# Batches of 10, 8 and 6 units, a fifth early unit of the last stage, and another way to fetch the fallback's rows

## The chip, the cores and the metric

One core of one Trainium2 chip runs the whole kernel in one launch. The metric is the device time of that launch in microseconds. Engines: TensorE (PE, its weight loads PEld), VectorE (DVE), ScalarE (ACT), GpSimd (POOL) and SyncE (SP), which issues the plain transfers; the indirect ones are issued by GpSimd.

## The reference, cut to what matters

```python
# 1 attention: B, H, S, D = 4, 8, 768, 48
for t in range(S):
    state = alpha[:, :, t, :, None] * state + np.einsum('bhd,bhe->bhde', k[:, :, t], v[:, :, t])
    y[:, :, t] = np.einsum('bhd,bhde->bhe', q[:, :, t], state)
# 2 experts on x, 3072 tokens of 384; 8 experts, 1024 hidden
do_compute = x @ w_skip > 0
xc = x[do_compute]; logits = xc @ w_gate; e_idx = np.argmax(logits, axis=1)
# gate_w: the softmax probability of e_idx
y[mask] = gate_w[mask, None] * (np.maximum(xc[mask] @ w1[e], 0.0) @ w2[e])   # for each e, mask = e_idx == e
out = x.copy(); out[do_compute] = xc + y
# 3 last stage on all tokens, 2048 hidden
h = x @ w_in; g = h - np.tanh(h); return g @ w_out
```

The weights of the last stage come in 64-bit floats, all else in 32-bit floats.

## The kernel before, in words

The kernel has three stages, attention, experts and last stage, in an order that is written out by hand: each engine runs its instructions in the order in which the lines below issue them, and waits on semaphores in that order. Nothing is replanned.

**Attention** goes over 24 units of 128 tokens (6 chunks of each of 4 sequences). Step s of `astep` works on several units: loads for s + 4, VectorE's two scans for s + 2 (`scanF`, `scanG`), the score product and its mask for s (`mmA`, `mask`), the output products of s - 1 (`mmYs`, `mmYa`), and the transposition of s - 2 back to token rows with its skip and gate logits (`evx`, `mmX`, `evxa`). Whatever else is to run beside a step is listed by step, in `at` (ahead of the step) and `aft` (behind its mask).

**Routing** is done for batches of units, 11, 9 and 4. `route1` (two pieces) finds the argmax, `route2` and `evr` count tokens ahead of each token on TensorE and copy the counts out, `route1b` fills gate and id, `route3` makes the row numbers (`loc`). `scatter(u)` then writes the unit's 128 rows with an indirect transfer into `xb`: 256 rows for each expert, then the tokens that skip the experts from the front of a second area and the others from its back.

**The transition.** The first 512 skipping tokens (`rload(0)`, step 21) need no expert. For them the last stage's first NE0 = 4 of 16 hidden units are computed between attention and the experts. `split2(0, a)` transposes 128 of those rows and splits them into two parts of TensorE's rounded 32-bit format, a high (ScalarE's cast) and a low one (VectorE's difference). Each weight unit is split in the same way: `wsplit` has two pieces for an expert's unit, and for the last stage's 64-bit weights five (s0 to s3): a mask-and-shift and a merge on VectorE, two ScalarE copies with a VectorE mask between, and three VectorE passes. All 64-bit units share one buffer (`raw64`). `mm1b` is a unit's first product (9 matmuls of 512 columns) and returns the steps behind it: tanh on ScalarE, g on VectorE, g's high part on ScalarE, its low part on VectorE. `mm2b` is the second product (12 matmuls of 384 columns). Between the units the first weights of expert 0 are split (RING0 = 4 buffers, loaded through three raw buffers).

**Experts.** 8 experts of 8 units each, `mm1` and `mm2`, with later weights loaded and split three to five units ahead. The same stage splits the last stage's units 4 to 9, which stay resident. **The last stage** runs the 12 other units for block 0 and all 16 for blocks 1 to 5, 92 steps, with the last NLATE = 6 weights split in its first steps.

**The fallback**, behind the last stage, is skipped unless an expert got over 256 tokens or too few tokens skip (`bounds`, `flag`). It computes every token anew from the rows fetched by `loc`.

Lines that the steps name: L235 score product, L240 mask, L256 output product, L303 and L311/L312 rows back and out, L155 to L176 split of 64-bit weights, L141/L144 split of expert weights, L386 and L393 rank product and its copy, L424 scatter, L438 rload, L446 to L449 transposes and splits, L473 and L507 the last stage's products, L479 to L485 tanh, g, high part, low part, L521 scatter to the output, L569 an expert's first product, L934 the skipped block, L1052 the end.

Of the kernel before, what the change touches and what calls it, by code (L numbers as in the profile page):

```python
# [39 lines left out]
RING = 8  # L40
LA = RING - 3
RAWS = 5
NE0 = 4
NLATE = 6

# [5 lines left out]
TOP = NS + N - 1  # L53
NROWS = NS + N
NCL = NE + 2
BATCHES = (11, 9, 4)
NB = max(BATCHES)
XW = PD + 9

# [2 lines left out]
def tile_kernel(ctx: ExitStack, tc: tile.TileContext, att0, att, vt, wsg, wmoe, wff, out):  # L62
# [229 lines left out]
    def evx(u):  # L292
        d = U[u]
        d["xT"] = rt.tile([PR, NP, C], F32, tag="xT", name=f"xT{u}")
        (V.tensor_copy if u == NU - 1 else A.copy)(d["xT"], d["py"])

    def mmX(u):

        d = U[u]
        d["px"] = (ps["T"].tile([128, NP, 128], F32, tag="X", name=f"px{u}") if u < NU - 1 else  # L300
                   ps["T"].tile([128, 2, NP, C], F32, tag="A", name=f"px{u}")[:, 0])
        for p in range(NP):
            T.matmul(d["px"][:, p, :XW], d["xT"][:, p], selw[:, p], start=p == 0, stop=p == NP - 1)  # L303
# [118 lines left out]
    def scatter(u):  # L422
        k, i = where[u]
        s_ = nc.gpsimd.indirect_dma_start(  # L424
            xb[:, :], bass.IndirectOffsetOnAxis(loc[:, u:u + 1], 0), RT[k]["xr"][:, i, :], None,
            bounds_check=NROWS - 1, oob_is_err=False)
        if u:
            tc.declare_no_dep(s_.ins, group="route", reason="rows of their own")
        tc.add_to_no_dep_group("route", s_.ins)
# [32 lines left out]
    def mm1b(nb, f, psum=psY):  # L462

        d = X2[nb]
        wh, wl = w_t[NMU + f]
        hp = psum(f"h2_{nb}_{f}")
        todo = [(w_[:, 128 * k:128 * k + 128], x_[:, k])
                for k in range(KT) for w_, x_ in ((wh, d["h"]), (wl, d["h"]), (wh, d["l"]))]
        last = len(todo) - 1

        def issue(n=len(todo)):
            for _ in range(min(n, len(todo))):
                T.matmul(hp, *todo.pop(0), start=len(todo) == last, stop=not todo)  # L473

        def after():
            g = rings["g"].tile([128, 512], F32, tag="g", name=f"g{nb}_{f}")
            gh = rings["g"].tile([128, 512], F32R, tag="gh", name=f"gh{nb}_{f}", bufs=3)
            gl = rings["g"].tile([128, 512], F32R, tag="gl", name=f"gl{nb}_{f}", bufs=3)
            A.activation(g, hp, AF.Tanh)  # L479
            yield  # L480
            V.tensor_tensor(g, hp, g, ALU.subtract)  # L481
            yield
            A.copy(gh, g)  # L483
            yield
            V.tensor_tensor(gl, g, gh.bitcast(F32), ALU.subtract)  # L485
            d["g", f] = (gh, gl)

        return issue, after
# [206 lines left out]
        at[s].append(lambda r0=r0: nc.sync.dma_start(  # L695
            xb[r0:r0 + 512, :].rearrange("(a p) d -> p a d", a=4), zero.unsqueeze(1).to_broadcast([128, 4, RW])))

    for k, (ld, s0) in enumerate(((1, 4), (6, 8), (12, 16), (19, 0))):
        at[ld].append(lambda k=k: wload(NMU + k))
        early = wsplit(NMU + k, fine=True)  # L700
        if s0:
            for s, f_ in zip((0, 1, 1, 2, 3), early):
                aft[s0 + s].append(f_)
    route = [route1(c) for c in range(len(BATCHES))]

    def advance(c):
# [2 lines left out]
    def rank(c, psum):  # L709
        route2(c, psum)  # L710
        evr(c)

    ranks = {first[1] + 3: 0, NU - 1: 1}
    for s, c, f_ in ((first[1] + 1, 0, advance), (first[1] + 2, 0, advance), (first[1] + 3, 0, route1b),
                     (first[1] + 4, 0, route3),
                     (NU - 3, 1, advance), (NU - 2, 1, advance), (NU - 1, 1, route1b), (NU - 1, 1, route3)):
        aft[s].append(lambda c=c, f_=f_: f_(c))
    for i in range(BATCHES[0]):
        aft[15 + (i + 1) // 2].append(lambda i=i: scatter(i))
    at[21].append(lambda: rload(0))  # L720

    def astep(s):

        def ok(u):
            return 0 <= u < NU

        def pX_(name):
            return ps["T"].tile([128, 512], F32, tag="X", name=name)

        if ok(s + 4):  # L730
            aload(s + 4)
        if ok(s + 3):
            vload(s + 3)
        for f_ in at[s]:
            f_()
        mmA(s)
        if ok(s - 2):
            evx(s - 2)
        if s in ranks:
            rank(ranks[s], pX_)  # L740
        if ok(s + 2):
            scanF(s + 2)
            mkqh(s + 2)
            scanG(s + 2)
            mkkh(s + 2)
            mkpf(s + 2)
        if ok(s - 1):
            mmYs(s - 1)
        trk(s)
        if ok(s - 1):  # L750
            evst(s - 1)
        evk(s)
        if ok(s - 2):
            mmX(s - 2)
            evxa(s - 2)
        mask(s)
        if ok(s - 1):
            mmYa(s - 1)
        for f_ in aft[s]:
            f_()  # L760
        mmS(s)
# [5 lines left out]
    p0 = pool("p0", 1)  # L767
    rings["x2", 0] = p0
    last = len(BATCHES) - 1
    aft[NU - 1].append(lambda: [scatter(u) for u in range(first[1], first[last])])  # L770
    for s in (NU - 2, NU - 1):
        a = 2 * (s - NU + 2)
        aft[s].append(lambda a=a: split2(0, a))
        aft[s].append(early[s - NU + 2])
        astep(s)
        split2(0, a + 1)


    def pX(name):
# [4 lines left out]
    mmYa(NU - 1)  # L784
    evx(NU - 1)
    mmX(NU - 2)
    evxa(NU - 2)
    mmX(NU - 1)
    evxa(NU - 1)
    early[2]()  # L790
    early[3]()
    att_ctx.close()
    rings["raw"] = pool("raws", 3, route_ctx, "right")
    part = p0.tile([128, 4, DM], F32, name="part")
# [17 lines left out]
    evr(last)  # L812
    route1b(last)
    route3(last)
    early[4]()
    for u in range(first[last], NU):
        scatter(u)
    psT_ctx.close()
    ps["A"] = pool("psA", 2, ps_ctx, space=bass.MemoryType.PSUM)
    next(fill[0])  # L820
# [1 line left out]
    more(psY)  # L822
    more(psS)
    for f in range(NE0):
        if 0 < f < NE0 - 3:
            more(psS)
        next(fill[f])
        next(fill[f])
        if f + 2 < NE0:
            next(fill[f + 2])  # L830
        next(fill[f], None)
        if f == NE0 - 1:
            for f_ in wsplit(f):
                f_()
            route_ctx.close()
            rings["ring2"] = pool("ring2", RING - RING0, moe_ctx, "right")
            rings["xe"] = pool("xe", 3, moe_ctx, "right")
            rings["m2"] = pool("m2", 2, moe_ctx, "right")
            rings["raw"] = pool("raws2", RAWS, moe_ctx, "right")
            xload(0)  # L840
            xload(1)
            wload(RING0)
            for a in range(2):
                xprep(0, a)
            for f_ in wsplit(RING0):
                f_()
        mm2b(0, f)
        if f < NE0 - 1:
            for f_ in wsplit(f):
                f_()  # L850
    blk0.close()
    at, aft = collections.defaultdict(list), collections.defaultdict(list)

# [80 lines left out]
    with tc.If(past > 0):  # L934
        xd = dp.tile([NU, 128, RW], F32, name="xd")
        xa = fp.tile([128, RW], F32, name="xa")
        for u in range(NU):
            nc.gpsimd.indirect_dma_start(xa, None, xb[:, :], bass.IndirectOffsetOnAxis(loc[:, u:u + 1], 0))
            nc.sync.dma_start(xd[u], xa)
        ecur = fp.tile([128, 1], F32, name="ecur")  # L940
        acc = fp.tile([128, DM], F32, name="acc")
        xTd = fp.tile([128, KT, 128], F32, name="xTd")
# [113 lines left out]
```

## Time and profile before

| | us |
|---|---|
| median of 3 runs | 725.51 (725.43 to 726.36) |
| the profiled execution | 726.17 |
| its span, first to last instruction | 724.5 |
| TensorE busy | 681.0 (94%) |
| VectorE, ScalarE, GpSimd busy | 439.4, 301.0, 144.1 |
| mean granted TensorE clock | 0.987 |

The page also cuts the span in 40 slices. TensorE's busy tenths are given in 40 digits on the page; below nine tenths are the first slice, four between 109 and 181 us, and the last. A busy TensorE is one with matmuls in flight; the ends of matmuls are modelled, so starts are the surer times. In the timeline the bracket behind a row says how long the engine had been idle and what ended that.

### The profile page before, as it was taken

How to read it: one execution, taken by the hardware profiler on the slowest of the kernel's cores; microseconds unless marked ns; L12 is line 12 of the kernel's file. 1: busy time of each engine (PE TensorE's matmuls, PEld its weight loads, DVE VectorE, ACT ScalarE, POOL GpSimd, SP SyncE). 2: the span in 40 equal slices, each digit the busy share in tenths (PEclk: the TensorE clock that was granted, in tenths of full speed). 3: DMA queues.
4: the chain of work that ended last, by engine and by line, in shares of the span. 5: the costliest groups of instructions: out<-in, count | busy, mean ns of one | idle time of the engine just before them, and what ended most of it. 6: DMA issues, size and time to landing. Idle time of an engine off the chain costs nothing.

```text
span 724.5 us, 11897 instructions
## 1 busy us (share of the span) xinstructions
PE 681.0 (94%) x4707; PEld 627.1 (87%) x4707; DVE 439.4 (61%) x712; ACT 301.0 (42%) x587; POOL 144.1 (20%) x145
## 2 busy tenths in 40 slices
PE   4999998868999999999999999999999999999993
PEld 3899997757999999989888999999989999999892
DVE  8999999756888888859943334333333343333331
ACT  2565563325666666525532333233323332333220
POOL 6665589250011111110011002000200020001002
PEclk9999999989999999999999999999999999999997
DMA  9999876347678877512210011001100110001001
GB/s 278 199 220 292 210 187 188 129 147 263 203 261 283 266 261 261 157 61 87 88 58 32 0 31 58 0 1 45 45 0 1 46 43 1 1 1 43 1 1 47
DMA packets 30543, 81.40 MB, mean 112 GB/s; under 512 B 4405, under 2 KB 14677, under 8 KB 30480
## 3 DMA queue, kind: packets, MB, share of 16 engines
q1 hardware_dynamic: 26384, 68.64, 32.1%
q0 software_dynamic: 4096, 11.92, 4.5%
q8 instruction: 39, 0.64, 0.4%
q14 instruction: 24, 0.20, 0.1%
HBM read 65.45 MB, written 15.84 MB: 112 GB/s over the span
## 4 chain that ended last, share of the span: by engine, by line
issue 52%; PE 17%; DVE 3%; POOL 2%; DMA 1%; ACT 0%; POOLq 0%; SPq 0%; ACTq 0%
PE hp L569 8%; PE yp L587 3%; PE yp L588 3%; PE yp L589 3%; POOL out_dram L521 2%; DVE wl L144 1%; PE pe L446 1%; DMA raw<-in_wmoe_dram 0%; DVE xe L596 0%; DVE ca L156 0%; DVE hl L574 0%; DVE ca L169 0%; DVE cl L165 0%; DVE el L449 0%; DVE cs L155 0%
## 5 line engine op out<-in xcount | busy, mean ns | idle before, releaser
L481 DVE TENSOR_TENSOR g<-h,g 128x512 f32<-128x512 f32 x96 | 66.3, 691 | 158.1 <-ACT g L479 149.8
L507 PE MATMUL y<-wh,gl 128*128 128x384 f32 x384 | 130.0, 339 | 0.1
L507 PE MATMUL y<-wh,gh 128*128 128x384 f32 x384 | 129.7, 338 | 0.4 <-ACT gh L483 0.4
L507 PE MATMUL y<-wl,gh 128*128 128x384 f32 x384 | 129.7, 338 | 0.0
L479 ACT ACTIVATE g<-h 128x512 f32<-128x512 f32 x96 | 57.3, 598 | 167.9 <-PE h L473 167.9
L473 PE MATMUL h<-xh,wl 128*128 128x512 f32 x288 | 114.2, 397 | 6.8 <-DVE wl L176 6.8
L473 PE MATMUL h<-xh,wh 128*128 128x512 f32 x288 | 115.6, 401 | 1.2 <-DVE g L481 1.2
L473 PE MATMUL h<-xl,wh 128*128 128x512 f32 x288 | 114.2, 396 | 0.0
L485 DVE TENSOR_TENSOR gl<-g,gh 128x512 fp32r<-128x512 f32 x96 | 66.5, 692 | 59.5 <-ACT gh L483 40.3
L521 POOL DMA_INDIRECT out_dram<-ob,id x24 | 23.7, 986 | 370.8 <-DVE ob L520 308.1
L483 ACT CAST gh<-g 128x512 fp32r<-128x512 f32 x96 | 59.6, 621 | 89.3 <-DVE g L481 89.3
L507 PEld LDWEIGHTS y<-wh,gh 128*128 128x128 f32 x384 | 72.1, 188 | 4.6 <-ACT gh L483 0.7
L507 PEld LDWEIGHTS y<-wl,gh 128*128 128x128 f32 x384 | 72.2, 188 | 4.2
L507 PEld LDWEIGHTS y<-wh,gl 128*128 128x128 f32 x384 | 72.1, 188 | 0.9 <-DVE gl L485 0.9
L473 PEld LDWEIGHTS h<-xh,wl 128*128 128x128 f32 x288 | 54.6, 190 | 16.3 <-DVE wl L176 7.6
L473 PEld LDWEIGHTS h<-xl,wh 128*128 128x128 f32 x288 | 54.5, 189 | 12.5
L141 ACT CAST wh<-raw 128x768 fp32r<-128x768 f32 x64 | 53.4, 835 | 26.7 <-PE yp L589 23.2
L473 PEld LDWEIGHTS h<-xh,wh 128*128 128x128 f32 x288 | 54.4, 189 | 10.3 <-DVE g L481 1.6
L144 DVE TENSOR_TENSOR wl<-raw,wh 128x768 fp32r<-128x768 f32 x64 | 60.7, 949 | 3.9 <-ACT wh L141 3.8
L569 PE MATMUL hp<-eh,wh 128*128 128x256 f32 x192 | 56.2, 293 | 3.8 <-DVE hl L574 3.8
L569 PE MATMUL hp<-el,wh 128*128 128x256 f32 x192 | 54.1, 282 | 0.2 <-DVE el L449 0.2
L569 PE MATMUL hp<-eh,wl 128*128 128x256 f32 x192 | 54.1, 282 | 0.0
(141 smaller groups left out, 1144.8 us busy)
## 6 DMA issues: line engine op xcount, KB each, us to landing
raw<-in_wmoe_dram SPq DMA_DIRECT2D x64, 384.0 KB
raw<-in_wff_dram SPq DMA_DIRECT2D x16, 768.0 KB
it<-in_att_dram SPq DMA_DIRECT2D x40, 289.5 KB
rows<-xb SPq DMA_DIRECT2D x6, 776.0 KB
vt<-in_vt_dram SPq DMA_DIRECT2D x24, 192.0 KB
xb<-zero SPq DMA_DIRECT2D x4, 776.0 KB
xe<-xb SPq DMA_DIRECT2D x8, 388.0 KB
it<-in_att_dram SPq DMA_DIRECT2D x2, 772.0 KB
```

The lines of the kernel that those rows point to most:

```text
L141: A.copy(t_["h"], raw_t[i])
L144: V.tensor_tensor(t_["l"], raw_t[i], t_["h"].bitcast(F32), ALU.subtract)
L473: T.matmul(hp, *todo.pop(0), start=len(todo) == last, stop=not todo)
L479: A.activation(g, hp, AF.Tanh)
L481: V.tensor_tensor(g, hp, g, ALU.subtract)
L483: A.copy(gh, g)
L485: V.tensor_tensor(gl, g, gh.bitcast(F32), ALU.subtract)
L507: T.matmul(o, g_[:, sl_], w_[:, DM:], start=first and n == 0, stop=last and n == len(todo) - 1)
L521: s_ = nc.gpsimd.indirect_dma_start(out[:, :], bass.IndirectOffsetOnAxis(d["id"][:, a:a + 1], 0), ob, None, bounds_check=N - 1, oob_is_err ...
L569: T.matmul(hp, w_[:, ks], x_[:, k], start=n == 0, stop=n == 3 * KT - 1)
L587: T.matmul(o, hh[:, sl_], wh[:, DM:], start=f == 0, stop=False)
L588: T.matmul(o, hh[:, sl_], wl[:, DM:], start=False, stop=False)
```

## The change

- The batches are 10, 8 and 6 units. Batch 0 is routed from step 11, batch 1 from step 19 to 22 with its first scatter in step 22 and the others in 23. `rank` of batch 1 stands in step 21.
- NE0 is 5 and NLATE 5: five units of the last stage are computed in the transition, and five are split late.
- The third early unit is loaded and split one step earlier. The fourth is loaded in step 17 and split in steps 22 and 23 (all of it in attention). The fifth is loaded behind attention and split between the units of the transition; expert 0's first three splits move behind the third and the fourth unit.
- The four `split2(0, a)` move from steps 22 and 23 behind attention, between the last units' row products. The last `xT` copy is ScalarE's.
- `mm1b` goes over its three terms in the outer loop and over k in the inner one.
- The fallback fetches its rows with plain transfers, one row at a time, in place of 24 indirect ones.

```diff
-NE0 = 4
-NLATE = 6
+NE0 = 5
+NLATE = 5
-BATCHES = (11, 9, 4)
+BATCHES = (10, 8, 6)
@@ evx
-        (V.tensor_copy if u == NU - 1 else A.copy)(d["xT"], d["py"])
+        A.copy(d["xT"], d["py"])
@@ mm1b
-                for k in range(KT) for w_, x_ in ((wh, d["h"]), (wl, d["h"]), (wh, d["l"]))]
+                for w_, x_ in ((wh, d["h"]), (wl, d["h"]), (wh, d["l"])) for k in range(KT)]
@@ lists of attention
-    for k, (ld, s0) in enumerate(((1, 4), (6, 8), (12, 16), (19, 0))):
+    early = [wsplit(NMU + k, fine=True) for k in range(NE0)]
+    for k, (ld, s0) in enumerate(((1, 4), (6, 8), (11, 15))):
         at[ld].append(lambda k=k: wload(NMU + k))
-        early = wsplit(NMU + k, fine=True)
-        if s0:
-            for s, f_ in zip((0, 1, 1, 2, 3), early):
-                aft[s0 + s].append(f_)
+        for s, f_ in zip((0, 1, 1, 2, 3), early[k]):
+            aft[s0 + s].append(f_)
+    at[17].append(lambda: wload(NMU + 3))
-    ranks = {first[1] + 3: 0, NU - 1: 1}
-    for s, c, f_ in ((first[1] + 1, 0, advance), (first[1] + 2, 0, advance), (first[1] + 3, 0, route1b),
-                     (first[1] + 4, 0, route3),
-                     (NU - 3, 1, advance), (NU - 2, 1, advance), (NU - 1, 1, route1b), (NU - 1, 1, route3)):
-        aft[s].append(lambda c=c, f_=f_: f_(c))
-    for i in range(BATCHES[0]):
-        aft[15 + (i + 1) // 2].append(lambda i=i: scatter(i))
+    for c in range(len(BATCHES) - 1):
+        s_ = first[c + 1] + 1
+        for n, f_ in enumerate((advance, advance, route1b, route3)):
+            aft[s_ + n].append(lambda c=c, f_=f_: f_(c))
+        ranks[s_ + 2] = c
+    for c in range(len(BATCHES) - 1):
+        for i in range(BATCHES[c]):
+            s_ = first[c + 1] + 4
+            aft[min(s_ + (i + 1) // 2, NU - 1)].append(lambda u=first[c] + i: scatter(u))
+    aft[NU - 2].append(early[3][0])
+    aft[NU - 1] += early[3][2:]
@@ astep, behind the rank product
+        if s == NU - 1:
+            early[3][1]()
@@ behind the steps
-    aft[NU - 1].append(lambda: [scatter(u) for u in range(first[1], first[last])])
-    for s in (NU - 2, NU - 1):
-        a = 2 * (s - NU + 2)
-        aft[s].append(lambda a=a: split2(0, a))
-        aft[s].append(early[s - NU + 2])
-        astep(s)
-        split2(0, a + 1)
+    astep(NU - 2)
+    astep(NU - 1)
...
     mmX(NU - 2)
+    split2(0, 0)
     evxa(NU - 2)
+    split2(0, 1)
     mmX(NU - 1)
     evxa(NU - 1)
-    early[2]()
-    early[3]()
+    split2(0, 2)
+    split2(0, 3)
+    wload(NMU + 4)
...
     route3(last)
-    early[4]()
     for u in range(first[last], NU):
         scatter(u)
+    early[4][0]()
...
     for f in range(NE0):
-        if 0 < f < NE0 - 3:
+        if f == 2:
+            for f_ in early[4][4:]:
+                f_()
             more(psS)
...
         mm2b(0, f)
-        if f < NE0 - 1:
-            for f_ in wsplit(f):
-                f_()
+        for f_ in ((early[4][1:2], early[4][2:4], wsplit(0), wsplit(1) + wsplit(2), ())[f]):
+            f_()
@@ fallback
-        for u in range(NU):
-            nc.gpsimd.indirect_dma_start(xa, None, xb[:, :], bass.IndirectOffsetOnAxis(loc[:, u:u + 1], 0))
-            nc.sync.dma_start(xd[u], xa)
+        locd = dp.tile([N, 1], U32, name="locd")
+        one = fp.tile([1, 1], U32, name="one")
+        nc.sync.dma_start(locd.rearrange("(u p) o -> p (u o)", p=128), loc)
+        with tc.For_i(0, N, 1) as ti:
+            nc.sync.dma_start(one, locd[bass.ds(ti, 1)])
+            row = nc.values_load(one[0:1, 0:1].bitcast(I32), engines=(mybir.EngineType.SP,), min_val=0,
+                                 max_val=NROWS - 1)
+            nc.sync.dma_start(xd.rearrange("u p d -> (u p) d")[bass.ds(ti, 1)], xb[bass.ds(row, 1), :])
```

## Rows read from the trace of the kernel before

**Rows 1.** Stretches (length, then busy us and instructions by engine, clock, DMA): last stage
```profile
325.00:350.00 25.00, 25.00 (x130) 22.66 (x129) 23.51 (x36) 12.06 (x20) 0.00 (x0) 1.00 0.29 95
```
**Rows 2.** Stretches, same columns (PE, PEld, DVE, ACT, POOL): the transition
```profile
149.90:156.00 6.10, 0.04 (x1) 0.04 (x1) 2.54 (x14) 1.19 (x3) 1.61 (x3) 0.70 0.17 66
156.00:169.80 13.80, 13.34 (x62) 11.38 (x62) 9.28 (x13) 7.25 (x12) 3.67 (x4) 0.89 0.42 144
...
176.40:180.00 3.60, 3.60 (x17) 3.60 (x17) 2.49 (x4) 2.01 (x4) 0.00 (x0) 0.55 1.01 399
```
**Rows 3.** Timeline, all engines, 135 to 165 us: start, us, engine, line, operation
```profile
147.20 0.24 PE L386 MATMUL pr<-oa,ones 128*128 128x40 bf16 x4
...
150.37 0.97 POOL L424 DMA_INDIRECT xb<-xr,loc  x1 [0.30 <-issue]
153.13 0.20 ACT L393 COPY prs<-pr 128x50 f32<-128x50 f32 x1 [8.14 <-remote]
...
155.96 0.79 PE L473 MATMUL h<-xh,wl 128*128 128x512 f32 x1 [6.10 <-DVE wl L176]
```
**Rows 4.** Timeline of VectorE, 153 to 176 us
```profile
155.82 0.69 DVE L481 TENSOR_TENSOR g<-h,g 128x512 f32<-128x512 f32 x1
...
159.28 0.68 DVE L481 TENSOR_TENSOR g<-h,g 128x512 f32<-128x512 f32 x1
...
167.89 0.96 DVE L144 TENSOR_TENSOR wl<-raw,wh 128x768 fp32r<-128x768 f32 x1
```
**Rows 5.** Timeline, all engines, 165 to 200 us: weight 4's load and split
```profile
168.92 5.60 SPq L122 DMA_DIRECT2D raw<-in_wmoe_dram  x6
...
172.34 0.83 ACT L141 CAST wh<-raw 128x768 fp32r<-128x768 f32 x1 [2.55 <-DMA raw<-in_wmoe_dram]
```
**Rows 6.** Timeline of GpSimd from 712 us on, the last scatter
```profile
713.75 0.98 POOL L521 DMA_INDIRECT out_dram<-ob,id  x1 [0.30 <-issue]
```
**Rows 7.** Line 934, the skipped block: count, ns min/median/max, first and last start
```profile
L934 POOLq EVENT_SEMAPHORE  x4: 17/43/43, 713.9 to 716.8; - x4
...
L934 POOLq INC_SWDGE_SEM  x1: 1464/1464/1464, 716.9 to 716.9; - x1
```
**Rows 8.** Line 1052, the end, same columns
```profile
L1052 SPq EVENT_SEMAPHORE  x14: 17/28/28, 718.3 to 724.4; - x14
...
L1052 POOLq DRAIN  x3: 45/107/5292, 718.3 to 724.2; - x3
L1052 SPq DRAIN  x3: 7/7/13, 719.0 to 723.9; - x3
```
**Rows 9.** The chain of waits: last output scatters of two blocks, 16 steps apart
```profile
381.57 0.98 POOL out_dram L521
...
449.27 0.98 POOL out_dram L521
```
**Rows 10.** Who waited for whom, 340 to 380 us: us in total, times, longest
```profile
PE h L473 <- DVE wl L176: 0.7, 1, 0.7
```
**Rows 11.** Timeline of TensorE, 123 to 146 us
```profile
125.98 1.16 PE L235 MATMUL pa<-qh,kh 64*128 64x128 f32 x16 [0.52 <-DVE am L240]
...
132.39 0.87 PE L446 MATMUL px<-ident,rows 128*128 128x128 f32 x6 [2.28 <-DMA rows<-xb]
...
139.27 1.08 PE L256 MATMUL py<-am,vt 128*48 128x128 f32 x16
...
142.94 0.48 PE L473 MATMUL h<-xh,wh 128*128 128x512 f32 x1
```
**Rows 12.** Stretches of VectorE alone: length, busy, clock, DMA
```profile
125.70:130.40 4.70, 3.92 (x15) 1.00 0.62 196
137.00:140.00 3.00, 2.79 (x21) 1.00 0.00 0
```
**Rows 13.** Groups of ScalarE, 132 to 144.5 us: busy us, mean ns, idle before
```profile
L448 ACT CAST xh<-px 128x384 fp32r<-128x384 f32 x4 | 1.8, 482 | 4.1 <-issue 3.1 <-PE px L446 0.9
```
**Rows 14.** Line 155, the mask-and-shift: count, ns min/median/max, first and last start
```profile
L155 DVE TENSOR_SCALAR cs<-raw x16: 549/552/1442, 33.2 to 355.9; 128x768 uint32<-128x768 uint32 x16
```

More of the change, by code (lines that the diff above doesn't have):

```diff
@@ L711, in rank @@
         evr(c)
-    ranks = {first[1] + 3: 0, NU - 1: 1}
-    for s, c, f_ in ((first[1] + 1, 0, advance), (first[1] + 2, 0, advance), (first[1] + 3, 0, route1b),
-                     (first[1] + 4, 0, route3),
-                     (NU - 3, 1, advance), (NU - 2, 1, advance), (NU - 1, 1, route1b), (NU - 1, 1, route3)):
-        aft[s].append(lambda c=c, f_=f_: f_(c))
-    for i in range(BATCHES[0]):
-        aft[15 + (i + 1) // 2].append(lambda i=i: scatter(i))
+    ranks = {}
+    for c in range(len(BATCHES) - 1):
[9 more added lines that the diff above has]
+    aft[NU - 1] += early[3][2:]
     at[21].append(lambda: rload(0))
@@ L832, in tile_kernel @@
         if f == NE0 - 1:
-            for f_ in wsplit(f):
+            for f_ in wsplit(RING0 - 1):
                 f_()
@@ L847, in tile_kernel @@
         mm2b(0, f)
-        if f < NE0 - 1:
-            for f_ in wsplit(f):
-                f_()
+        for f_ in ((early[4][1:2], early[4][2:4], wsplit(0), wsplit(1) + wsplit(2), ())[f]):
+            f_()
     blk0.close()
```

## The prediction

> **What bounds the kernel now.** I read the page's busy shares and its slices first: TensorE is busy 94% of 724.5 us, and nearly all that it is not lies between 120 and 180 us, before 20, and after 712. From 325 us on it has no idle time at all [rows 1]: there only less TensorE work helps. So two places are open: the transition from attention to the experts, and the end.
>
> In the transition the table of stretches shows 6.1 us in which TensorE does nothing, at a granted clock that falls to 0.70 and stays at 0.89 in the next stretch; a later 3.6 us stand at 0.55 [rows 2]. The timeline says why. TensorE finishes the last batch's rank product at 147.44, but ScalarE copies it out only at 153.13, "remote", 8.1 us idle: the signal came late, from nothing that the profile shows. Behind that copy VectorE's ranks of the last batch and then the low half of the fourth early unit stand in order, and TensorE waits 6.1 us for that half, at 155.96 [rows 3]. From there VectorE and ScalarE hand each other g, its high part, its low part and a weight split: 3.46 us a unit (155.82 to 159.28), where TensorE needs some 2.1 us for a unit's second product. The fourth weight split of expert 0 ends at 168.85 [rows 4]; the load of weight 4 is issued right behind, lands at 172.3, and ScalarE stands before it with the first relu behind it [rows 5].
>
> At the end, the last scatter is issued at 713.75 and done by 716.8. Then GpSimd raises the semaphores of the skipped block's indirect transfers for 1.46 us, and drains for 5.29 us; SyncE is through at 719.1, and everybody waits for that drain [rows 6 to 8].
>
> **The change, part by part.** Sums are made against the profiled execution (726.17 us, span 724.5); the median of the runs is 0.66 lower, and the forecast is lowered by as much.
>
> *Fallback.* The 24 indirect gathers go, so nothing of GpSimd's queues is left in the skipped block; nothing else of it runs. What goes is the raise (1.46). Whether the 5.29 us drain goes is not shown. Bounds: gone, as long as the other two drains of GpSimd (0.05 and 0.11 us) [rows 8]; or still 5.29, from when the last scatter leaves GpSimd (713.75 + 0.98 = 714.73) or from its landing (716.8). What is late next is the last scatter's landing at 716.8, then SyncE's row of waits (718.3 to 719.0 today, 0.7), then what stands behind the drain today (724.5 - 718.3 - 5.3 = 0.9): end at 716.8 + 0.7 + 0.9 = 718.4, a gain of 6.1. With the drain kept: 714.73 + 5.29 + 0.9 = 720.9, gain 3.6, or 716.8 + 5.29 + 0.9 = 723.0, gain 1.5. Nothing gained is the end on the other side (the raise stays), and a loss would need a wait that the block doesn't get. I take 6.1: the long drain stands directly behind the raise, all scatters had landed 1.5 us before it, and the nearest rows without a raise are short.
>
> *A fifth early unit.* It takes one of 92 steps out of the last stage. Steps there cost (449.27 - 381.57) / 16 = 4.23 us [rows 9], and TensorE is full: -4.23. The reordered first product asks for the low weights three matmuls later, 3 x 0.23 us; the last stage has one wait for such a half, 0.7 us [rows 10], which goes. One late unit less also takes some 5 us of VectorE from the stage's start, where it is busy 23.5 of 25 us [rows 1]; that frees nothing on TensorE, counted 0. Elsewhere the order costs nothing: each matmul loads its own weights either way. Sum -4.9.
>
> *Attention.* Batches of 10 and 8 bring batch 0's routing and scatters and the third early unit's split one step earlier, and batch 1's routing from steps 21 to 23 to 19 to 22. TensorE's waits there name VectorE's mask [rows 11], so VectorE's work is not free: the first two route pieces now stand before unit 21's mask. Today they run between 125.7 and 130.4, 3.92 us busy, of which 1.2 is a mask: 2.7 us [rows 12]. Two fewer scatters beside steps 19 and 20 give about 1 us of that back, so step 22 starts 1.6 us later than 125.98. In return the wait of 2.3 us for the rows goes (the load is issued at the same step, but its transposes stand two steps later), and so do twelve transposes between the steps. TensorE's own work from step 22 to the last attention product is 2 x 4.15 + 2.15 = 10.5 us: the product ends at 138.2 instead of 139.27 + 1.08 = 140.35 [rows 11]. VectorE has 2.8 us of ranks, 2.4 of split and 1.2 of mask to do before it, from about 130.1: 136.5 at the latest, hidden.
>
> The last xT goes from VectorE to ScalarE (0.68 to 0.60), beside a product. Then the four splits of the tokens stand here, in ScalarE's queue with two evictions of 0.19 + 0.49 each: product 1.04, transposes 0.45, four casts of 0.48 [rows 13], two evictions, 4.75 us to the first unit, against 142.94 - 140.35 = 2.6 today. 138.2 + 4.75 = 142.95: no shift. Bounds: -2 (VectorE keeps TensorE's pace as today) to +2.5 (the whole 2.7 + 2.2 minus the 2.3 wait).
>
> *Transition.* Rank product again at 147.4. I take its signal as prompt, as the other two rank products' were (ScalarE's idle time before their copies, 1.8 and 0.4 us, ends with the product): copy at 147.5, not 153.13. Ranks 1.8 us, then the first piece of the fifth unit's split, 1.45 us, in place of the 0.87 of the low half: g starts 3.3 us behind the copy, 150.8, 5.0 us earlier. Behind it the chain is longer: a fifth unit (3.46 - 0.87 = 2.6) and the fifth unit's four other vector pieces (0.55 + 3 x 0.87 = 3.2), less some 0.8 that fall into the 0.7 us gaps in which VectorE waits for the cast: +5.0 (bounds 3.2, all of the unit in gaps, to 6.7). The fourth weight split ends at 150.8 + 13.0 + 5.0 = 168.8, as today; weight 4's load, its wait and the slow clock behind it stay. Shift 0, -3 to +3.
>
> VectorE's mask-and-shift, which opens each split, took 0.55 us alone and up to 1.44 [rows 14]; those beside GpSimd's transfers are the long ones. The Trainium skill ("SBUF — State Buffer", "Who interferes with whom") says that such an instruction and a GpSimd one take the shared port pair in turns, the later one blocked for all of it. By that rule the split behind the six scatters costs 0.9 more, and the time would be 715.4; the trace agrees on who is slowed, not on which of the two comes first here.
>
> New waits: weight 3's load now waits for weight 0's split, three units in (about 162), and xe's loads stand behind it on SyncE; six scatters instead of four end near 158, so they are not late; xe is there at 166, before its transposes. The eight scatters of batch 1 run from 132 to 142 instead of 140 to 151.
>
> Sum: -6.1 - 4.9 + 0 = -11.0; 726.17 - 11.0 - 0.66 = 714.5 us.
>
> **Rivals.** *The drain is not the raise's.* Then it stays 5.29: 717.0 or 719.1. For it: a drain is an instruction of its own, and 24 scatters stood before it; against: they had landed. 17%.
>
> *The late signal comes back.* Its release falls near the landing of batch 1's ninth scatter (150.37 + 0.97, and 2.1 more from issue's end to landing as at the end: 153.4) [rows 3, 6, 7]. If it is bound to the last batch instead of that scatter, 5.6 us return before g: 720.1. Against: the scatters now land by 144. 13%.
>
> *The block keeps its raise*, because the skip still settles all queues: no gain at the end, 720.6. The diff leaves no GpSimd transfer in the block. 6%. That the block would run is excluded: in the reference's data the first ten units hold 646 tokens that skip, and 512 are asked of them.
>
> *Slower: signals of TensorE are held as long as a run of scatters is in flight.* Then eight scatters from 132 hold the last attention product's signal from 138.2 to 143.8 (+5.6), and six more, then 155 to 162.5 and landed at 164.6, hold the third unit's from 157.8 (+6.8); each stop brings a stretch at about half clock as in [rows 2] (3.6 us at 0.55: +1.6 each). 714.5 + 15.6 = 730.1. It turns slower when holds pass 11.0 us. Against: four scatters from 155.5 held nothing, and signals passed while the first three of the nine were out. 6%.
>
> **Numbers.** The forecast case has 58%. Its own range is 711 to 718 (transition -3 to +3). To the 80% belong the kept drain and one late signal, and both ends of the attention bounds: 711 to 721. A change of 0.2%, 1.5 us, is about what can be told from none. Slower: the hold, 6%, and 1% for an unseen cost; no change: kept drain with a late signal and a transition at its upper bound, 3%; faster 90%.
>
> **What would show it.** Right: no GpSimd semaphore raise in the profile's block line and a GpSimd drain under 0.5 us at the end, last instruction about 4 us behind the last scatter; 91 steps in the last stage; ScalarE's third rank copy within 0.5 us of the product; no wait for a low half over 0.3 us; the load of weight 4 near 169. Wrong: a drain of 5 us; "remote" idle on ScalarE; g to g over 4 us in most units, with experts starting past 172; step 22 later than 128.5.

## The result and the profile after

| | before | after |
|---|---|---|
| median, this comparison (4 runs each) | 725.88 us (725.43 to 726.36) | 719.49 us (718.69 to 720.42) |
| ratio, 95% interval | | 0.9911 [0.9896, 0.9927] |
| median, a later comparison (17 and 12 runs) | 719.79 us (718.76 to 724.94) | 719.55 us (717.67 to 722.20) |
| ratio, 95% interval | | 0.9991 [0.9973, 1.0009] |
| profiled execution, span | 726.17, 724.5 us | 720.42, 718.6 us |

In the first comparison the kernel after is faster by 6.4 us where the prediction said 11.0; in the later one the two can't be told apart. The kernel after takes the same time in both. It is the kernel before that differs: in the later one 14 of its 17 runs lie at 718.8 to 720.6 us, as fast as after, and three at 722.5 to 724.9. What the forecast counted as a fixed cost of the old order is one that not every execution pays. How many pay it differs between comparisons, each on another chip: in two of those below the fastest of 17 runs took over 723 us.

The end first, in the timeline of GpSimd and in the rows of line 940 (the skipped block) and 1063 (the end). Columns as in [rows 7].

```profile
711.45 0.97 POOL L521 DMA_INDIRECT out_dram<-ob,id  x1 [0.30 <-issue]
...
L940 POOLq COMPARE_BRANCH  x1: 45/45/45, 711.1 to 711.1; - x1
...
L1063 POOLq DRAIN  x3: 45/113/6472, 711.3 to 718.3; - x3
L1063 SPq DRAIN  x3: 7/7/13, 715.4 to 718.0; - x3
```

The raise of [rows 7] is gone, and so is the wait for the last scatter's landing. The drain is still there. It is issued at 711.3, ahead of the scatter's start, and ends at 717.8, 5.4 us behind the moment the scatter left GpSimd (711.45 + 0.97 = 712.42). From the last scatter's start to the end of the span it is 7.1 us now, 10.7 before.

Then the transition, in timelines of single engines; they answer [rows 3 to 5].

```profile
148.63 0.30 PE L386 MATMUL pr<-oa,ones 128*128 128x60 bf16 x6
148.97 0.22 ACT L393 COPY prs<-pr 128x70 f32<-128x70 f32 x1 [2.85 <-PE pr L386]
150.91 0.55 DVE L155 TENSOR_SCALAR cs<-raw 128x768 uint32<-128x768 uint32 x1
...
152.40 0.68 DVE L481 TENSOR_TENSOR g<-h,g 128x512 f32<-128x512 f32 x1
...
165.16 0.45 PE L507 MATMUL y<-wh,gh 128*128 128x384 f32 x1 [1.36 <-ACT gh L483]
...
168.38 0.85 PE L446 MATMUL pe<-ident,xe 128*128 128x128 f32 x6 [0.48 <-DMA xe<-xb]
...
170.75 6.35 SPq L122 DMA_DIRECT2D raw<-in_wmoe_dram  x6
171.68 0.38 PE L569 MATMUL hp<-eh,wh 128*128 128x256 f32 x1
...
174.93 0.83 ACT L141 CAST wh<-raw 128x768 fp32r<-128x768 f32 x1 [3.31 <-DMA raw<-in_wmoe_dram]
177.14 0.40 ACT L573 ACTIVATE hh<-hp 128x256 fp32r<-128x256 f32 x1
178.07 0.48 PE L569 MATMUL hp<-eh,wh 128*128 128x256 f32 x1 [3.57 <-DVE hl L574]
```

ScalarE copies the ranks right behind the product: no "remote" (idle time that ends by nothing the profile shows; a **late signal** below). From there the chain of units is longer, the experts start at 171.68 (169.84 before), and then TensorE stands still for 3.57 us. The rows say why: ScalarE's first relu (177.14) stands in its queue behind the cast of weight 4, which waits for a load issued only at 170.75. The kernel before had the same wait, 2.80 us long, in its timeline of TensorE:

```profile
169.84 0.39 PE L569 MATMUL hp<-eh,wh 128*128 128x256 f32 x1
...
175.48 0.39 PE L569 MATMUL hp<-eh,wh 128*128 128x256 f32 x1 [2.80 <-DVE hl L574]
```

The stretches of after's execution show the price behind it, the granted clock at about half:

```profile
0.00:20.00 20.00, 9.01 (x82) 7.71 (x82) 16.61 (x30) 5.89 (x13) 13.26 (x24) 0.86 0.85 258
...
174.00:178.00 4.00, 0.50 (x5) 0.30 (x3) 2.21 (x5) 3.07 (x6) 0.00 (x0) 1.00 1.02 326
178.00:182.00 4.00, 3.93 (x17) 3.93 (x18) 3.37 (x6) 1.65 (x4) 0.00 (x0) 0.57 0.90 334
```

The first of these rows is an accident of the profiled execution. Its clock was 0.86 in the first 20 us (1.00 in the profile before), and by step 5 it is 0.93 us late, in a part that the change doesn't touch. A second profile of after, from the later comparison (719.22 us), has a clock of 1.00 there and copies the ranks at 147.48.

### The profile page after: what moved, and what is told of

It is laid out like the page before. It is cut to its first block, busy times and chain, and to the rows that moved or that the text cites. A ratio compares the mean times of both kernels' runs of the same rounds, so it can differ in the third digit from the quotient of the medians.

```text
span 718.6 us, 11890 instructions
## 1 busy us (share of the span) xinstructions
PE 681.6 (95%) x4707; PEld 626.0 (87%) x4707; DVE 439.9 (61%) x711; ACT 301.2 (42%) x588; POOL 147.0 (20%) x145
## 4 chain that ended last, share of the span: by engine, by line
issue 52%; PE 18%; DVE 3%; POOL 2%; DMA 1%; ACT 0%; POOLq 0%; SPq 0%; DVEq 0%
PE hp L569 9%; PE yp L587 3%; PE yp L588 3%; PE yp L589 3%; POOL out_dram L521 2%; DVE wl L144 1%; PE pe L446 1%; DMA raw<-in_wmoe_dram 1%; DVE xe L596 0%; DVE ca L156 0%; DVE cl L165 0%; DVE hl L574 0%; DVE ca L169 0%; POOLq L1063 0%; DVE cs L160 0%
## 5 line engine op out<-in xcount | busy, mean ns | idle before, releaser
L473 PE MATMUL h<-xh,wh 128*128 128x512 f32 x288 | 84.3, 401 | 1.7 <-DVE g L481 1.2
L473 PE MATMUL h<-xl,wh 128*128 128x512 f32 x288 | 82.5, 395 | 0.0
L473 PE MATMUL h<-xh,wl 128*128 128x512 f32 x288 | 82.2, 394 | 0.0
L473 PEld LDWEIGHTS h<-xh,wh 128*128 128x128 f32 x288 | 51.5, 188 | 7.0 <-DVE g L481 1.8
```

## The experiments

Medians of before were 726.5, 726.4, 721.3 and 719.8 us in the four comparisons, on different chips. So kernels of different comparisons are set side by side by stretches of their traces, one profiled execution each: the **tail** (last scatter's start to the end of the span), the **chain** (rank copy to first expert product) and the **rest** (first expert product to last scatter). The start of the copy also holds what attention took in that execution.

| kernel | median, ratio to before there | copy | chain | rest | tail |
|---|---|---|---|---|---|
| before | 725.88 | 153.13 | 16.7 | 543.9 | 10.7 |
| after | 719.49, 0.991 | 148.97 | 22.7 | 539.8 | 7.1 |
| before, plain fallback | 721.24, 0.991 | 154.07 | 16.7 | 543.8 | 7.1 |
| after, first relu ahead | 713.66, 0.981 | 149.02 | 22.7 | 534.8 | 7.1 |
| after, four early units | 715.56, 0.986 | 147.15 | 19.6 | 538.9 | 7.1 |
| four units, relu ahead | 713.95, 0.990 | 148.96 | 18.0 | 538.5 | 7.1 |
| before, relu ahead | 716.80, 0.993 | 151.99 | 18.0 | 539.0 | 11.7 |
| relu ahead, low halves between | 711.41, 0.981 | 148.65 | 20.0 | 534.1 | 7.1 |

### The end

**The fallback alone**, put into the kernel before:

```diff
-        for u in range(NU):
-            nc.gpsimd.indirect_dma_start(xa, None, xb[:, :], ...)
-            nc.sync.dma_start(xd[u], xa)
+        with tc.For_i(0, N, 1) as ti:
+            ...
+            nc.sync.dma_start(xd.rearrange("u p d -> (u p) d")[bass.ds(ti, 1)], xb[bass.ds(row, 1), :])
```

> The kernel before, with the fallback's gathers alone replaced by plain transfers; batches, early units and order as before. Theory A (read from the trace of after): the raise and the wait for the last scatter's landing go, the drain of 5.3 us stays and is counted from the moment the last scatter leaves GpSimd, so the end stands 7.1 us behind the last scatter's start in place of 10.7: -3.6 us, about 722.3. Theory B (the forecast): the drain belongs to the raise and shrinks below 0.5 us: -6.1, about 719.8. Theory C: the shorter tail of after comes from other parts of the change, not from the fallback: 0.

Measured: 721.24 us, ratio 0.9914 [0.9882, 0.9946]; tail 7.1. The row of the end:

```profile
L1057 POOLq DRAIN  x3: 45/112/6470, 714.4 to 721.4; - x3
```

Theory A by the trace: the fallback is worth 3.6 us, and the drain stays, to 5.3 us behind the scatter. The ratio says somewhat more (5.3 us); why is not shown. This profile has the rank product 4.5 us later than before's and its signal 2.1 us late instead of 5.7, so it copies 0.9 us later.

**What the drain hangs on.** The last block's rows go out by plain stores:

```diff
+        if nb == NU // 4 - 1:
+            nc.sync.dma_start(out[512 * nb + 128 * a:512 * nb + 128 * a + 128, :], ob)
+            return
```

> The kernel after, but the last block's four output scatters are replaced by plain stores on SyncE's queue (the block's rows are stored in the order in which they stand, so the last block's output rows are in other places). The last transfer that GpSimd issues is then a scatter of the block before, some 60 us earlier. Theory A: the drain's 5.3 us run from the last scatter that GpSimd issued: long over, the drain is short, and the end is set by the last store's landing, about 713, plus 1.6: span near 714.5, -4 us against after. Theory B: the drain costs 5.3 us wherever GpSimd has scattered at all: it starts at GpSimd's branch, about 710.5, and ends at 715.8, span 716.7, -1.9 us. Theory C: a drain waits for the landing of transfers on any queue plus a fixed time: no gain.

Measured: 716.59 us. Lines 943 (block) and 1066 (end):

```profile
L943 SPq EVENT_SEMAPHORE  x9: 17/17/17, 714.5 to 715.1; - x9
...
L943 SPq COMPARE_BRANCH  x1: 50/50/50, 710.9 to 710.9; - x1
...
L1066 POOLq DRAIN  x3: 45/113/7146, 651.0 to 716.6; - x3
L1066 SPq DRAIN  x3: 7/7/13, 716.0 to 716.3; - x3
```

Theory A holds for the drain: it runs from 651.0 to 658.1, 5.0 us behind the last scatter that GpSimd issued (652.19 + 0.97), and is over 58 us before the end. But the span shrinks by 1.7 us instead of 4; that theory B's 1.9 comes near is chance, since its drain would have run to 715.8. SyncE, which in after passes the branch at 566.4, now takes it behind the last store, at 710.9, and its next instruction runs at 714.5: 3.6 us that no theory had. Whether they are the skip's or the last store's landing is not shown; in after, 4.7 us pass there, also right behind a transfer (issued at 566.0), and cost nothing.

The lengths fit one more reading, which no run tested alone. The kernels with 64 indirect transfers drain for 5.29 us behind the raise or until 5.2 to 5.5 us behind the last scatter, the one above with 60 until 5.0, and the kernel before without nine of its scatters (below), with 55, for 4.56 us behind the raise: about 0.083 us for each transfer that the kernel has issued.

### The late signal

**Batch 1's scatters later**, behind the copy of the last attention product:

```diff
+    G.tensor_tensor(hold, xl_[:, 0, 0:2], xl_[:, 0, 2:4], ALU.mult)
+    for u in range(first[1], first[2]):
+        scatter(u)
```

> The kernel after, but batch 1's eight scatters start behind the copy of the last attention product (140.5 in place of 132), by a small GpSimd instruction that reads it: they run to about 151 and land by 153.5, so they are in flight when the last batch's rank product ends at 148.8, as nine were in the kernel before. Theory A: the signal of a TensorE product is held until scatters in flight have landed: ScalarE's rank copy starts at 153 to 154 in place of 148.97 and its idle time before it ends by 'remote'; g starts 4.5 us later, the expert stage 3 to 4.5 us later, 722.5 to 724. Theory B: the late signal of the kernel before had to do with that kernel's order, not with scatters in flight: the copy stays within 0.5 us of the product; only the last six scatters move 1.3 us later and xe with them, 719.5 to 721.

Measured: 723.62 us. Timelines of TensorE, GpSimd and ScalarE:

```profile
148.60 0.30 PE L386 MATMUL pr<-oa,ones 128*128 128x60 bf16 x6
150.31 0.97 POOL L424 DMA_INDIRECT xb<-xr,loc  x1 [0.30 <-issue]
152.74 0.22 ACT L393 COPY prs<-pr 128x70 f32<-128x70 f32 x1 [6.67 <-remote]
```

Theory A: moving the scatters alone brings the late signal back, to 1.5 us behind the eighth scatter's end; all ten runs lie at 721.84 us or above. In before it ended 1.8 us behind the ninth (151.34 to 153.13), in the run with the plain fallback 1.3 us behind the ninth. TensorE, 4.4 us idle for the first high part, then ran 4.8 us at half clock, and the experts started at 176.61.

**Later still**, behind a piece of the last batch's routing:

```diff
+    a_ = RT[last]["ac"]
+    G.tensor_tensor(hold, a_[:, 0:2], a_[:, 2:4], ALU.mult)
+    for u in range(first[1], first[2]):
+        scatter(u)
```

> The kernel after, but batch 1's eight scatters start behind VectorE's piece at 146.9 (by a small GpSimd instruction that reads it): they run from about 147.7 to 158, with the last batch's six behind them if its rows are ready. When the rank product ends at 148.9 only the first of them is in flight. Theory A: what holds a TensorE signal is any back-to-back run of scatters in flight, to its end: the copy starts when the eighth has landed, 159 to 160, the longest hold of all, time 729 to 731. Theory B: products that end in a run's first 3 us pass, as those at 142 and 143 passed in the run from 141.3: the copy at 149, g as in after; only xe comes 6 to 7 us later, time 724 to 727.

Measured: 719.43 us, one run. Timelines of GpSimd and ScalarE:

```profile
146.46 1.01 POOL L424 DMA_INDIRECT xb<-xr,loc  x1 [0.57 <-issue]
147.47 0.22 ACT L393 COPY prs<-pr 128x70 f32<-128x70 f32 x1 [2.85 <-PE pr L386]
...
160.03 0.60 ACT L479 ACTIVATE g<-h 128x512 f32<-128x512 f32 x1 [0.55 <-PE h L473]
```

Theory A falls: this is the longest run of scatters, fourteen from 146.5 to 166.2, and a product's signal passes through its middle, at 160.0. Theory B had the copy right and the rows late (TensorE waits 4.9 us for them), but not the time: weight 4's load was no longer late behind that wait.

**Without that run of scatters**, in the kernel before:

```diff
-    aft[NU - 1].append(lambda: [scatter(u) for u in range(first[1], first[last])])
-    for s in range(6, 6 + NS // 512):
+    for s in range(6, 6 + NROWS // 512):
```

> The kernel before without batch 1's nine scatters (their rows are left out of the result; the rows that they would have written are filled with the same empty rows as the expert region, by six more fills early in attention). Theory A: the run of scatters holds the rank product's signal: without it ScalarE's rank copy starts within 0.5 us of the product (near 147.5 in place of 153.13), no idle time ends by 'remote', g starts near 150.2 in place of 155.8, and the expert stage 4 to 5 us earlier, about 165: 717 to 721 us. Theory B: the late signal has another cause in that stretch (the order, the weight loads): the copy still starts 3 to 6 us behind the product, 724 to 726 us.

Measured: 731.07 us, but attention was 13.8 us longer in its profile (its last product starts at 153.03 in place of 139.27), so the time says nothing. The copy starts 0.1 us behind the product, as theory A had it. That is no proof. The kernel before with the first relu moved (below) has the old order and all nine scatters, from 144.42 to 155.8, and its profiled execution has a prompt copy too. Timelines of TensorE and ScalarE:

```profile
151.66 0.24 PE L386 MATMUL pr<-oa,ones 128*128 128x40 bf16 x4
151.99 0.20 ACT L393 COPY prs<-pr 128x50 f32<-128x50 f32 x1 [2.72 <-PE pr L386]
```

So the late signal was seen only with a back-to-back run of scatters in flight, and it comes in some executions and not in others. The rank product's ended 1.3 to 1.8 us behind the run's last scatter. Other products' came late inside a run: with the plain fallback VectorE's last copy of attention rows waited for one until 145.25 (scatters from 140.95 to 152.78), and the run with batch 1's rank product one step later (below) shows two more. What decides is open.

**After once more**, over more executions:

> The kernel after, unchanged, over more executions beside the kernel before. Theory A: with batch 1's scatters done at 145.5 no product that VectorE waits for through ScalarE ends late in a run of scatters, so no execution has a late signal: all executions between 718 and 721.5 us, while those of before spread over 5 us or more. Theory B: the late signal only became rarer: some executions of after at 723 us and above.

Measured: 719.55 us, 717.67 to 722.20 in 12 runs; before 719.79. Theory A's times nearly hold for after (two runs lie just outside its bounds, none at 723). Its reason doesn't hold for after's placing of the scatters: the run with batch 1's rank product one step later (below) has the same one, and late signals. Neither theory had that most runs of before would be as fast. That these are the runs without the late signal fits the sums: without its 5.6 us the two profiles differ by 0.2, and the medians here by 0.24. But none of these runs was profiled: it is inferred, and a late signal is not all that slows before. In the profile with the prompt copy at 151.99, the slowest of its eight runs (722.47 us), VectorE waits 4.4 us for an attention load (1.2 at most in before), and the rank product itself starts only at 151.66.

### The fifth unit and the order behind it

**Four early units** in the kernel after:

```diff
-NE0 = 5
-NLATE = 5
+NE0 = 4
+NLATE = 6
```

> The kernel after with four early units instead of five (six late ones; weight splits 0, 1, 2 behind the first three units, as in the kernel before); batches and fallback as in after. The last stage has one step more: +4.9 us. Theory A: the expert stage can't start earlier for it, since the rows of expert 0 land only at 168.4 in after (their load stands behind weight 3's, which waits for weight 0's split): first expert product near 169.5 instead of 171.7, the wait for weight 4's load as long as before: net +2.5 us, about 722. Theory B (the forecast's sum): the fifth unit costs 5 us of the chain from the rank copy on, so without it the experts start at 166.7 and all is even: 719.5. Theory C: the wait behind weight 4's load grows by what the start gains, so the early start is lost: +4.5 us, 724.

Measured: 715.56 us, 3.9 less than after's in its own comparison, and chain and rest are 4.0 us shorter; no theory had it. Timelines of SyncE and TensorE:

```profile
162.18 5.51 SPq L122 DMA_DIRECT2D raw<-in_wmoe_dram  x6
162.51 1.51 PE L446 MATMUL pe<-ident,xe 128*128 128x128 f32 x6 [2.38 <-DMA xe<-xb]
166.79 0.28 PE L569 MATMUL hp<-eh,wh 128*128 128x256 f32 x1
...
169.38 0.39 PE L569 MATMUL hp<-eh,wh 128*128 128x256 f32 x1 [0.29 <-DVE hl L574]
```

With one unit less the splits are through while TensorE waits for expert 0's rows. Weight 4's load goes out at 162.18, and the 3.57 us are 0.29. The fifth unit takes its 4.9 us out of the last stage, and pays with a chain 3.1 us longer and with a stall and a half clock that would have gone.

**The first relu ahead of weight 4's split**, in after:

```diff
-            for f_ in wsplit(RING0):
-                f_()
+    for f_ in wsplit(RING0):
+        at[2].append(f_)
-        stage(j, s_, max(0, s_ - RAWS + 1))
+        stage(j, s_ + 2, max(0, s_ - RAWS + 1))
```

> The kernel after, with weight 4's split moved from ahead of the first expert's first relu to the third step of the expert stage, and the splits of the weights behind it two steps later each; the loads stand where they stood. Theory A (order on ScalarE): TensorE's 3.57 us of idle time before the product at 178.07, and the 3.4 us at half clock behind it, exist only because the first relu stands behind a cast that waits for weight 4's load (landed 174.9): both go, -3.6 to -5.3 us, 714.2 to 715.9. Theory B (supply): the weights behind weight 4 are as late as it is, so the wait comes back two to four steps on, before the product of weight 4 or 5: no more than 1 us gained, 718.5 to 719.5. Theory C: with splits two steps later in the whole expert stage the low halves come late, slower than after by over 2 us.

Measured: 713.66 us, ratio 0.9811 [0.9781, 0.9840]. The same stretches as above:

```profile
174.00:178.00 4.00, 4.00 (x31) 3.93 (x31) 2.70 (x5) 2.22 (x4) 0.00 (x0) 1.00 0.93 307
178.00:182.00 4.00, 4.00 (x31) 3.97 (x30) 2.05 (x5) 2.82 (x6) 0.00 (x0) 1.00 0.90 322
```

Theory A: the rest is 4.95 us shorter, and no other stretch changed by more than 0.1.

**The same move in before**, and with four units (the same diff):

> The kernel before, with the first relu ahead of weight 4's split and nothing else of the change. Theory A: TensorE's 2.80 us before 175.48 and the two stretches at half clock behind it (3.6 us in all) go, as in the kernel after: -3 to -4.6 us, ratio 0.994 to 0.996. Theory B: the kernel before has slack elsewhere that takes it up: within 0.7 us of before.

> Four early units (as in the run with 715.56 us) and the first relu ahead of weight 4's split (as in the run with 713.66 us). Theory A: with four units weight 4's load is on time already (issued at 162.2 while TensorE waits for expert 0's rows; the wait behind it is 0.29 us), so the order gives nothing: 0 to -0.6 us against 715.56, and the fifth unit is worth 1.3 to 2 us once the order is mended. Theory B: the order is worth the same 5 us here, 710.5, and the fifth unit is a loss under both orders.

Measured: 716.80 us against 721.3 there, 0.9932 [0.9907, 0.9958], rest 4.9 us shorter: theory A, at its upper end. (The chain is 1.3 us longer; TensorE waits 1.4 us in it for expert 0's rows.) So one moved split gives the kernel before about three quarters of what the whole change gave in its better comparison (0.9911), on another chip. With four units 713.95 us: rest 0.4 us shorter, as theory A said of the order. What it said of the fifth unit, 1.3 to 2 us, failed: with the order mended, five units have 3.7 us less in the rest than four and 4.7 more in the chain, and the fifth earns nothing.

**Low halves between**, on top of the moved relu (`between` holds the low halves of weights 0 and 1 and one piece of the fifth unit's split):

```diff
+        for f_ in between[f]:
+            f_()
         next(fill[f], None)
...
-    rings["raw"] = pool("raws", 3, route_ctx, "right")
+    rings["raw"] = pool("raws", 4, route_ctx, "right")
```

> The kernel with the first relu ahead of weight 4's split (713.66 us), and three edits more: VectorE's low halves of weights 0 and 1 stand between g and its low part, in the 0.7 us in which VectorE waits for ScalarE's cast; one vector piece of the fifth unit's split likewise; and the raw weights have four buffers in place of three, so that weight 3's load no longer waits for weight 0's split and the load of expert 0's rows behind it starts when the scatters have landed, about 162 in place of 164.6. Theory A: the chain of units is VectorE's and ScalarE's, and the rows come in time: first expert product 169 to 170 instead of 171.7, -1.7 to -2.7 us, 711 to 712. Theory B: only one of the two moves, and the other (the rows at 168.4, or the chain) sets the start as before: 0 to -0.5 us. Theory C: the rows' load now waits for a later piece of VectorE's: +1 to +3 us.

Measured: 711.41 us, 0.9810 [0.9776, 0.9844], the fastest kernel of this study. Timelines of SyncE and TensorE:

```profile
161.37 0.89 SPq L548 DMA_DIRECT2D xe<-xb  x2
165.73 0.82 PE L446 MATMUL pe<-ident,xe 128*128 128x128 f32 x6
168.63 0.39 PE L569 MATMUL hp<-eh,wh 128*128 128x256 f32 x1
```

Theory A, 0.4 us earlier than it said: chain 20.0 instead of 22.7. Which of the three edits gave how much is not told apart. Against four units with the relu ahead it is 2.0 us more in the chain and 4.4 less in the rest, so with this chain five units come out ahead; four units with these edits were not run.

**Batch 1's rank product one step later:**

```diff
-        ranks[s_ + 2] = c
+        ranks[s_ + 2 + c] = c
```

> The kernel after, with the rank product of batch 1 one step later in TensorE's order, so that TensorE no longer waits 1.34 us at 125.71 for VectorE's choice of experts. Theory A: in those steps VectorE is the bound (18.7 of 20 us busy from 120 to 140), so TensorE only waits elsewhere, for the mask: within 0.3 us of after. Theory B: the wait is on the path: -1.3 us.

Measured: 721.06 us, 717.3 to 728.6: too wide to tell. The timeline and a stretch of TensorE in the profiled run (725.62 us) say that theory B is wrong:

```profile
127.62 1.54 PE L235 MATMUL pa<-qh,kh 64*128 64x128 f32 x16 [2.14 <-DVE am L240]
...
127.60:131.60 4.00, 3.98 (x35) 3.78 (x36) 3.25 (x16) 0.24 (x1) 0.11 (x1) 0.58 0.01 4
```

TensorE waits for the mask instead, longer, and runs 4 us at 0.58 behind it. From step 5 to step 23 it is 100.7 us, 99.2 in after: theory A's cause, 1.5 us above its bound.

That is not what makes this execution long. Step 23 starts at 133.49, 133.55 in after, but the last rank product at 153.98 in place of 148.63. Between them stand late signals, with batch 1's eight scatters in flight from 132.21 to 143.35. Timelines of TensorE and ScalarE:

```profile
138.64 1.08 PE L256 MATMUL py<-am,vt 128*48 128x128 f32 x16
142.66 0.59 ACT L295 COPY xT<-py 128x512 f32<-128x512 f32 x1 [3.09 <-PE px L446]
144.13 0.48 ACT L448 CAST xh<-px 128x384 fp32r<-128x384 f32 x1 [0.88 <-remote]
```

ScalarE copies the last attention product 2.9 us behind its end (0.1 in after), and the first tokens' transposes, through at 141.45, wait until 144.13. VectorE stands idle for 5.9 us, and TensorE's clock is 0.53 from 145 to 150. Seven other profiled executions with these eight scatters beside the last attention products have no such wait. So the new order is not free of late signals; whether the moved rank product has a part in it is not shown.

## Why the prediction was right and where it failed

The time (719.49) lies in the range, the sign is right, the size is 58% of the forecast. That is so against the executions of before that had the late signal, and to be set against those was luck: in the later comparison the change gives 0.2 us. Step by step, from the two profiled executions:

| step | forecast | measured |
|---|---|---|
| start to step 5 | 0 | +0.9 |
| to the last attention product | -2.15 | -1.5 |
| to the first unit | +2.15 | +2.0 |
| to the rank copy | -5.6 | -5.6 |
| copy to first expert product | +5.6 | +6.0 |
| weight 4's wait | 0 | +0.75 |
| the last stage | -4.9 | -4.9 |
| the tail | -6.1 | -3.6 |
| around the span | 0 | +0.15 |
| sum | -11.0 | -5.8 |

**The tail** is the step that failed: "I take 6.1". Half of the miss is here. The nearest rows were two drains of 0.05 and 0.11 us; they stand behind the long one, so they were no measure of a first drain without a raise. The bound of 3.6, drain counted from the scatter's leaving GpSimd, is what came, to 0.1 us. The argument against that rival, that all scatters had landed, had no weight: in before the drain ran 5.3 us from the raise, in after and in the plain-fallback run to 5.4 and 5.3 from the scatter, in the plain-store run to 5.0.

**The fifth early unit** came to the digit in the last stage: 711.45 - 178.07 = 533.4 us against 713.75 - 175.48 = 538.3, and the wait of 0.7 us for a low half is gone. (That wait makes "no idle time at all" from 325 us on too strong: TensorE is busy 24.26 us of the 25 from 350.)

**Attention** was 0.65 us short. VectorE is the bound, 18.7 of 20 us from 120 to 140 (15.9 before). I had not seen that TensorE would wait 1.34 us at 125.71 for VectorE's choice ahead of batch 1's rank product; the run with batch 1's rank product one step later shows that this wait is only a place for VectorE's lateness. The third early unit's last low half took 2.93 us at 111.69, beside GpSimd's two products of 1.29 and 1.28 (1.90 before). The Trainium skill ("SBUF — State Buffer", "Who interferes with whom") says that a VectorE instruction with two inputs in SBUF contends with a GpSimd one that reads SBUF. The trace agrees: 0.95 alone. The mask-and-shift behind the scatters, for which the prediction gave 0.9 us, started at 150.91, before the first of them, and took 0.55. Its row was misread: the long ones stand beside GpSimd's products, not its transfers (in before, 1.44 us at 97.69 beside a product at 97.43), and one beside a scatter in after, at 133.60, took 0.55.

**The transition** came out in its sum for the reason given: the signal was prompt, the chain as much longer. What failed is what the sum was set against. "Weight 4's load, its wait and the slow clock behind it stay" is true of after, but the wait belonged to the late chain. With the signal prompt and no fifth unit it goes (0.29 us), so the fifth unit, set at 5.0 us of chain against 4.9 of gain, cost some 9: without it the chain is 3.1 us shorter, and the rest 0.9 in spite of the step that comes back. And the -5.6 holds only against an execution that had the late signal. "I take its signal as prompt, as the other two rank products' were" was right of both profiles of after. That before would have it late in every execution was taken from one profile and never asked.

**The marks.** No raise, 91 steps, copy within 0.1 us of the product, no wait for a low half: right. Wrong: the drain of 6.5 us, step 22 at 129.48 (128.5 was the limit; 0.9 of it is the slow start, and the second profile of after has 127.98), weight 4's load at 170.75 in place of 169. Of the rivals "the drain is not the raise's" came true (17%). The rival of held signals (6%) names something real, even the product whose signal came late in the run with batch 1's rank product one step later, but not its condition: not every run of scatters holds one.

## What to carry to other kernels

Before a wait in a profile is priced as a term, ask whether it belongs to the order or to that execution: a wait that ends by nothing that the profile shows may be absent from the next run, and then what removes it gains nothing. Look in each in-order queue for an instruction that waits for a transfer and has the critical path's next one behind it; here one moved split gave 5 us. With the stall of 3.6 us at TensorE went 1.4 more, of the half clock behind it.

## What the runs showed of the hardware

- GpSimd's first drain at the end ran until 4.6 to 5.5 us behind its last indirect transfer or semaphore raise in all profiles, and was shorter where the kernel had issued fewer such transfers (4.56 us for 55, 5.29 for 64). Where the last transfer lay 58 us before the end, it cost nothing.
- From SyncE's branch over the block to its next instruction it was 3.6 us when it came last (710.9 to 714.5).
- The last rank product's signal reached ScalarE 5.7, 3.8 and 2.1 us late in three profiled executions with a run of scatters in flight, and promptly in two others with such a run; in a further one the last attention product's came 2.9 us late.
